# A gated long convolution and an MLP: the sequence in two halves, each transformed modulo x^1024 - i, with MLP pieces of the first half written between convolution pieces of the second

## The chip, the cores and the metric

The kernel runs on one core of a Trainium2 chip. The core has a matrix engine (TensorE, in the profile PE, with its weight loads as PEld), a vector engine (VectorE, DVE), a scalar engine (ScalarE, ACT), a general engine (GpSimd, POOL), an engine that mostly starts transfers (SyncE, SP), and 16 DMA engines. Each engine works through its own instruction list in order, and semaphores tie the lists together. Matrix products land in PSUM, eight banks of 128 x 512 fp32 values; everything else lives in SBUF, 128 partitions wide.

The metric is the device time of one launch in microseconds, as the median of several runs. The profile comes from one execution, of which it records the span from the first to the last instruction.

## The reference

The input sequence has S = 2048 positions of D = 512 channels. Two kinds of layer alternate, four layers in all, with a residual around each and a layer norm in front:

```
A(q, k, v): k_shift[s] = sum over t of k[s-t] * shift_k[:, 3-t..]   (4 taps per channel)
            kv = k_shift * v
            y  = causal convolution of kv with ssm_k (length 2048), by FFT of length 4096
            y  = y + kv * ssm_D
            return q * y
B(x):       h = gelu(layernorm(x) @ w1 + b1);  return h @ w2 + b2      (F = 1376)

x = A_q
x = x + A(layernorm(x), k, v);  x = x + B(layernorm(x))
x = x + A(layernorm(x), k, v);  x = x + B(layernorm(x))
```

k, v and the filters are the same in both A layers and do not depend on x, so y is computed once and used twice: an A layer is then only `x + layernorm(x) * y`. B normalises once more, so between two MLPs each row goes through two layer norms and one gating product.

## The kernel before

The convolution is written as a transform modulo x^2048 - i. A real sequence of 2048 values becomes 1024 complex ones of a twisted transform, which gives the causal (linear) convolution without padding. A transform of 2048 = 32 x 64 has two matrix stages: stage one multiplies by the table `Ft` (`first_stage`, L320, matmul L327), then 16 x 2 transposes per chunk of 128 channels turn the result (L344), and stage two multiplies by `Wt` (L381 for the filter, L448 for kv). The filter's spectrum lies in `ZK`, and a copy with real and imaginary halves swapped in `KSW`, made by eight SBUF-to-SBUF transfers of 512 KB (`sa..`, `sb..`). VectorE multiplies the spectra (pieces `T`, L459, two products at once in a 128 x 2048 instruction), TensorE goes back with the table `Mt` (pieces `V`, L471), transposes (pieces `TP`, L515) and `GPt` (pieces `Y`, L493) into `YA`. A sequence chunk cc is 128 of the 512 channels; filter pieces are named K, those of kv U, X, T, V, TP and Y.

In front of this k is transposed (pieces `kT`, L405), and the 4-tap shift is done as matmuls against diagonal matrices `DG` (pieces `kv`, L421, 32 matmuls for 8 rows x 4 taps; pieces `kvm` multiply by v, L427). The diagonals are made on GpSimd (pieces `dg0` to `dg3`, L398, 16 instructions in all) from the tap table `sF`, a cast of `sT`, which a small transfer on ScalarE's queue brings (L194). The filter is transposed into token order too (pieces `KT`, L367).

The MLP works on groups of 512 positions (GT = 4 rows of 128), four groups per layer. `mm1` (L609) does 11 x 4 matmuls of 512 columns into one PSUM bank after the other, each emptied by a gelu on ScalarE (L617) into `hT`; `mm2` (L619) does 4 x 11 matmuls, each result added to x by VectorE (L628); in the last layer each row tile is then stored. `prep` (L283) does the layer norm, gating and second layer norm of a later group on VectorE and GpSimd, writes the result to DRAM from the GpSimd queue (L293) and reads it back transposed on the SP queue (L294) into `lnT`.

The order of the convolution and of the layer norms of the first two groups is a list written out by hand, `ORDER`: each word is a piece, its engine (P TensorE, D VectorE, A ScalarE, G GpSimd, S the SP queue) and its buffer numbers. `_Plan.write` emits the pieces in that order; each engine runs its own pieces in the order of the list. `p0` to `p3` are four PSUM tiles of two banks. After the list comes the MLP in plain loops, over groups 0 to 7 in the order mm1 of group i, `prep` of group i + 2, mm2 of group i - 1:

```
for i, (l, g) in enumerate(seq):
    mm1(ns[i])
    if i < len(seq) - 2:
        ns[i + 2] = prep(seq[i + 2][1])
    ...
    if prev is not None:
        mm2(ns[prev], seq[prev][1], seq[prev][0] == 1)
    prev = i
```

A transfer from the SP or ScalarE queue counts on one of eight semaphores, in turn, so the ninth such transfer waits until the first has landed.

Of the kernel before, what the change touches and what calls it, by code (L numbers as in the profile page):

```python
# [17 lines left out]
KT2.P1 dt1.D K1S0.P20 KT2e.D KT3.P3 K1S0e.A dg2.G dt2.D K1S1.P0 KT3e.D K1S2.P1 K2S0.P21 K1S2e.A KT0.P3 K1S1e.D  # L20
K2S0e.A dt3.D K2S3.P1 KT0e.D K2S2.P0 K2S3e.A kT0.P2 dt0.D K2S2e.A K2S1.P3 kT0e.D kT3.P1 K2S1e.A K3S0.P02 kT3e.D
kT1.P2 K3S0e.A K3S1.P3 kT1e.D K3S2.P1 K3S1e.A K2T0.P0 K3S2e.A K1S3.P2 K2T0e.D K2T1.P3 K1S3e.A K3S3.P1 K2T1e.D
K0S0.P01 K3S3e.A K1T0.P2 K0S0e.D K0S1.P3 K0S3.P1 K0S1e.A K1T0e.D K1T1.P0 K0S3e.A K0S2.P3 K1T1e.D K3T0.P2 kT2.P1
K0S2e.D K3T1.P0 kT2e.A lM.S K3T0e.D K0T0.P3 K3T1e.D K210.P2 kv21.P1 K210e.A K0T0e.D K200.P0 kvm21.D K216.P2
K200e.A kv30.P3 K216e.A K217.P1 kvm30.D K213.P0 K217e.A kv20.P2 K213e.A K211.P3 kvm20.D K202.P1 kv00.P0 K202e.A
K211e.D K201.P2 kvm00.D kv01.P1 K201e.A U0S0.P30 kvm01.D K203.P0 U0S0e.A U0S1.P2 K0T1.P1 K203e.D U0S1e.A U0S3.P3
K0T1e.D sa00.S U0S2.P0 sb00.S U0S3e.A kv10.P2 U0S2e.D K212.P1 kvm10.D K204.P3 K212e.A U2S0.P02 K207.P2 U2S0e.D
K204e.A U0T0.P1 sb10.S sa10.S K207e.A K215.P3 U0T0e.D K214.P0 kv31.P2 K214e.A K215e.D K205.P1 sa11.S kvm31.D
sb11.S U2S1.P0 K205e.A U0T1.P3 U2S1e.A X00.P20 U0T1e.D K206.P1 X00e.A X01.P01 K206e.D U2S3.P3 kv11.P2 X01e.A
T00.D0 sa01.S U2S3e.A sb01.S U2S2.P1 T01.D1 V00.P01 U2S2e.A X02.P32 kvm11.D V00e.A V01.P1 X03.P20 X02e.A V01e.D  # L30
U2T0.P0 X03e.A U3S0.P30 U2T0e.D U2T1.P1 U3S0e.A U3S3.P2 U2T1e.D X20.P01 U3S3e.A U3S2.P3 U3S1.P1 X20e.D U3S2e.A
U1S0.P22 U1S0e.D U1S2.P0 U3S1e.A U1S3.P3 U1S1.P1 U1S2e.A T20.D2 U3T0.P2 U1S1e.A T03.D0 X22.P01 U1S3e.A U3T1.P1
U3T0e.D V20.P30 X22e.A U3T1e.D V03.P2 V20e.A X30.P00 T22.D1 V03e.A U1T0.P1 T02.D2 X30e.A X23.P31 U1T1.P2 X23e.A
U1T0e.D V02.P0 U1T1e.D X31.P32 V02e.A V22.P1 T30.D0 X31e.A lx.S TP00.P2 V22e.A T23.D2 X13.P00 V30.P32 X13e.A
T31.D1 X11.P11 V23.P0 V30e.A TP00e.D X11e.A X21.P32 T13.D0 V31.P2 X21e.A Y00.P1 T11.D2 V23e.A X33.P30 T21.D1
V31e.A X32.P01 TP08.P2 X32e.A s10.D Y00e.A X10.P02 X10e.A V21.P1 TP08e.A T10.D1 s11.G X12.P02 s00.D X33e.A
V10.P21 X12e.A Y08.P3 V10e.A V11.P0 Y08e.A V13.P2 T12.D1 s01.G V11e.A V21e.D V12.P3 V13e.A T32.D2 TP20.P0 V12e.A
T33.D0 V32.P1 TP10.P2 TP20e.D V32e.A w1.S w3.S w2.S w4.S V33.P3 TP10e.D Y20.P1 V33e.A s02.D Y10.P0 Y20e.A
TP30.P2 TP18.P3 Y10e.A TP30e.D TP28.P1 s12.A ga.D Y30.P2 TP34.P0 gs.D Y30e.A TP18e.A TP38.P2 gl0.D TP34e.A
Y18.P3 gl2.D TP38e.A gp00.G Y34.P0 Y34e.D gp02.G gb00.A h2.D Y38.P0 gb02.D Y18e.A LT00.P2 h0.D LT00e.A LT02.P3  # L40
LT02e.A hs2.D TP28e.A hs0.D gp12.G Y38e.A Y28.P2 gb12.A gp10.G Y28e.D gb10.A
"""
NA, NB = 32, 64
# [8 lines left out]
def _make_tables():  # L52
    a = np.arange(NA)
    k1 = np.arange(NA)
    psi = 2 * np.pi * np.outer(a, k1 + 0.25) / NA

    F = np.zeros((128, 2, 128))
    G = np.zeros((128, 2, 128))
    for x in range(2):
        for bh in range(2):  # L60
            rows = 4 * a + 2 * bh + x
            F[rows, x, bh * 64:bh * 64 + 32] = np.cos(psi)
            F[rows, x, bh * 64 + 32:bh * 64 + 64] = np.sin(psi)
            for i, p in enumerate(rows):
                G[bh * 64:bh * 64 + 32, x, p] = np.cos(psi[i]) / 64
                G[bh * 64 + 32:bh * 64 + 64, x, p] = np.sin(psi[i]) / 64
    b = np.arange(NB)
    k2 = np.arange(NB)
    W = np.zeros((128, NA, 128))
    M = np.zeros((128, NA, 2, 128))  # L70
    for k in range(NA):
        phi = 2 * np.pi * (((k + 0.25) * b / 2048)[:, None] + np.outer(b, k2) / NB)
        c, s = np.cos(phi), np.sin(phi)
        for bh in range(2):
            cb, sb = c[bh * 32:bh * 32 + 32], s[bh * 32:bh * 32 + 32]
# [12 lines left out]
    W = W[32 * (p % 4) + 16 * (p // 4 % 2) + p // 8]
    GP = G[32 * (p % 4) + p // 4]
    return tuple(_to_bf16_uint16(t) for t in (F, G, GP, W, M))  # L90


class _Plan:
# [3 lines left out]
    def __init__(self, rings):  # L97
        self.rings = rings
        self.items = []

    def add(self, name, cost, deps, fn, take=(), free=(), nbytes=0, last=0):
        it = dict(name=name, cost=cost, deps=[d for d in deps if d is not None], fn=fn, take=list(take), slot={},
                  free=list(free), nbytes=nbytes, last=last)
        self.items.append(it)
        return it

    def write(self, order):
        pieces = {it["name"]: it for it in self.items}
        assert len(pieces) == len(self.items)
        for word in order.split():  # L110
            name, how = word.split(".")
            it = pieces.pop(name)
            it["eng"] = how[0]
            it["slot"] = {ring: int(c) for ring, c in zip(it["take"], how[1:])}
            it["fn"](it)
        assert not pieces
# [3 lines left out]
def kernel(ctx: ExitStack, tc: tile.TileContext, A_q, A_k, A_v, A_shift_k, A_ssm_k, A_ssm_D,  # L120
                 B_x, B_w1, B_b1, B_w2, B_b2, out):
    nc = tc.nc
# [4 lines left out]
    NT = S // P  # L127
# [3 lines left out]
    TOK = "(p nt) d -> p nt d"  # L131
    q_d, k_d, v_d, out_d = (t.flatten_outer_dims() for t in (A_q, A_k, A_v, out))
    K = 1024
    NZT, NTB = 3, 3
# [5 lines left out]
    F_np, G_np, GP_np, W_np, M_np = _make_tables()  # L140
    F_h = nc.inline_tensor(F_np, name="tabF")
    G_h = nc.inline_tensor(G_np, name="tabG")
    GP_h = nc.inline_tensor(GP_np, name="tabGP")
    W_h = nc.inline_tensor(W_np, name="tabW")
    M_h = nc.inline_tensor(M_np, name="tabM")

# [4 lines left out]
    ROW = 149 * K // 2  # L151
# [3 lines left out]

        return apf(arena, p0 * ROW + off // 2, [[ROW, n]] + dims)

    def place(name, shape, off):
# [7 lines left out]
    ZK = place("ZK", [P, 2, NA, D // 2], 0)  # L166
    ZX = place("ZX", [P, 2, NA, D // 2], 32 * K)
# [37 lines left out]
    def chunk(t, c):  # L205

        return t[:, c // 2, :, c % 2 * CW:c % 2 * CW + CW]
# [469 lines left out]
```

## Time and profile before

| | |
|---|---|
| median of three runs | 278.88 us (278.71 to 278.91) |
| span of the profiled execution | 277.7 us |
| TensorE busy | 257.6 us, 93% of the span, 2208 matmuls |
| VectorE busy | 187.0 us, 67% |
| ScalarE busy | 153.8 us, 55% |
| GpSimd busy | 41.1 us, 15% |
| data moved by DMA | 27.48 MB |

The profiled execution lasted 277.7 us from its first to its last instruction, and the median of the runs is 1.2 us above that span. In the page's slices a digit is the busy share of a fortieth of the span (6.9 us) in tenths; PEclk is the granted clock of TensorE in tenths of full speed. A row of the chain of waits is start, duration and what ran; because the matmuls are pipelined, the durations in the chain are paces, while the mean of a single matmul in the groups is its latency. A row of the table of stages gives the stage, its length, the busy time of each engine with the number of instructions, the granted clock, the share of DMA time and the rate. A row of the timeline is start, duration, engine, line, operation, tiles and count, with the idle time before it in brackets.

### The profile page before, as it was taken

Reading aid. Unit: us, or ns where it says so; the run is one execution under the profiler, and the core shown is the slowest. Engines: PE = TensorE matmul, PEld = TensorE weight load, DVE = VectorE, ACT = ScalarE, POOL = GpSimd, SP = SyncE. Lnnn points to the kernel's source line nnn. Section 1 sums busy time; section 2 is a strip of 40 time slices with the busy share of each in tenths; the row PEclk is TensorE's granted clock in tenths of the full one; section 3 lists DMA queues with packets and bytes.
Section 4 is the critical chain, followed back from the end, with each engine's and each line's share of the span. In section 5 each row is a group of like instructions: output and inputs, shape, how many; then the busy total and the mean of one; then the engine's idle time right before and its main releaser. Section 6 shows DMA issues by size and latency. Waiting matters only on the chain.

```text
span 277.7 us, 5353 instructions
## 1 busy us (share of the span) xinstructions
PE 257.6 (93%) x2208; PEld 168.6 (61%) x2208; DVE 187.0 (67%) x346; ACT 153.8 (55%) x186; POOL 41.1 (15%) x73
## 2 busy tenths in 40 slices
PE   3979999999997994589999999999999999999994
PEld 3969999998997994535444444444444444444441
DVE  0959767799999999995857875886777720110221
ACT  1566655788899889798751713705507217036000
POOL 3490000000002402313020121111111200000000
PEclk9999999999999999779999999999999999999999
DMA  7993703994800083000523023023040070110111
GB/s 234 308 402 148 293 14 76 225 216 94 304 2 2 2 295 113 1 2 9 143 76 78 0 77 76 4 76 76 2 130 21 6 210 13 38 38 2 39 55 58
DMA packets 21164, 27.48 MB, mean 99 GB/s; under 512 B 13874, under 2 KB 17684, under 8 KB 19988
## 3 DMA queue, kind: packets, MB, share of 16 engines
q1 hardware_dynamic: 19522, 23.93, 29.2%
q0 software_dynamic: 944, 3.15, 3.5%
q8 instruction: 17, 0.28, 0.4%
q10 hardware_dynamic: 674, 0.07, 0.2%
q14 instruction: 7, 0.06, 0.1%
HBM read 14.56 MB, written 5.24 MB: 71 GB/s over the span
## 4 chain that ended last, share of the span: by engine, by line
PE 76%; DVE 13%; DMA 5%; ACT 2%; issue 2%; ACTq 0%; POOL 0%; DVEq 0%
PE po L625 27%; PE ph L615 26%; DMA sT<-in_A_shift_k_dram 3%; PE p_121 L421 3%; DMA arena<-in_A_k_dram 2%; PE p_120 L344 2%; DVE lst_105 L241 2%; DVE T_95 L459 2%; PE p_121 L344 1%; PE p_119 L344 1%; PE p_120 L421 1%; PE p_122 L327 1%; PE p_122 L344 1%; DVE arena L535 1%; DVE arena L427 1%
## 5 line engine op out<-in xcount | busy, mean ns | idle before, releaser
L617 ACT ACTIVATE arena<-ph,B_73 128x512 bf16<-128x512 f32 (+1 forms) x88 | 60.2, 687 | 71.0 <-PE ph L615 71.0
L615 PE MATMUL ph<-arena 128*128 128x512 bf16 (+1 forms) x352 | 79.1, 385 | 1.1 <-ACT arena L617 1.1
L625 PE MATMUL po<-arena 128*128 128x512 bf16 (+1 forms) x352 | 77.7, 379 | 0.0
L615 PEld LDWEIGHTS <-arena 128*128 128x128 bf16 (+1 forms) x352 | 35.6, 101 | 43.3 <-issue 3.6
L625 PEld LDWEIGHTS <-arena 128*128 128x128 bf16 (+1 forms) x352 | 34.3, 98 | 40.9
L628 DVE TENSOR_TENSOR arena<-po,arena 128x512 bf16<-128x512 f32 x32 | 22.0, 687 | 50.8 <-PE po L625 50.8
L421 PEld LDWEIGHTS <-arena 128*128 128x128 bf16 x256 | 15.0, 98 | 0.2
L223 ACT ACTIVATE arena<-p_120 128x1024 bf16<-128x1024 f32 (+1 forms) x8 | 10.0, 1248 | 6.5 <-PE p_120 L381 4.7
L327 PEld LDWEIGHTS <-arena 128*128 128x128 bf16 x128 | 11.9, 99 | 1.9 <-issue 0.4
L225 DVE COPY arena<-p_119 128x2048 bf16<-128x2048 bf16 x6 | 7.3, 1221 | 7.8 <-PE p_119 L367 6.7
L493 PEld LDWEIGHTS <-GPt 128*128 128x128 bf16 x128 | 8.0, 102 | 6.5 <-issue 3.8
L241 DVE BATCH_NORM_STATS2 lst_105<-arena 128x6 f32<-128x512 bf16 (+2 forms) x20 | 11.2, 579 | 0.3
L223 ACT ACTIVATE arena<-p_121 128x1024 bf16<-128x1024 f32 (+3 forms) x8 | 9.5, 1187 | 3.3 <-PE p_121 L381 1.7
L225 DVE COPY arena<-p_121 128x2048 bf16<-128x2048 bf16 (+1 forms) x9 | 10.4, 1160 | 1.0 <-PE p_121 L515 0.6
L241 DVE BATCH_NORM_STATS2 lst_109<-arena 128x6 f32<-128x512 bf16 x16 | 10.8, 685 | 0.3
L225 DVE COPY arena<-p_120 128x2048 bf16<-128x2048 bf16 x7 | 8.6, 1221 | 3.0 <-PE p_120 L405 2.0
L596 POOL MEMSET arena<- 1x512 bf16 x2 | 1.0, 519 | 61.5 <-PE p_122 L448 61.5
L241 DVE BATCH_NORM_STATS2 lst_101<-arena 128x6 f32<-128x512 bf16 x16 | 9.9, 679 | 0.1
L241 DVE BATCH_NORM_STATS2 lst_97<-arena 128x6 f32<-128x512 bf16 x16 | 9.9, 678 | 0.1
L250 POOL TENSOR_TENSOR lrs_107<-lrs_107,mhalf 128x4 f32<-128x4 f32 (+1 forms) x5 | 4.9, 975 | 33.5 <-DVE lnm_108 L247 33.5
L398 POOL TENSOR_SCALAR DG<-IDt,sF 128x128 bf16<-128x128 bf16 x16 | 9.3, 607 | 0.1
L250 POOL TENSOR_TENSOR lrs_103<-lrs_103,mhalf 128x4 f32<-128x4 f32 x4 | 5.0, 1246 | 26.8 <-DVE lnm_104 L247 26.8
(161 smaller groups left out, 400.5 us busy)
## 6 DMA issues: line engine op xcount, KB each, us to landing
arena<-arena SPq DMA_DIRECT2D x8, 512.0 KB, 8.3
arena<-in_A_ssm_k_dram SPq DMA_DIRECT2D x4, 512.0 KB, 5.0
arena<-in_A_k_dram SPq DMA_DIRECT2D x4, 512.0 KB, 7.1
arena<-in_A_v_dram SPq DMA_DIRECT2D x2, 1024.0 KB, 11.5
arena<-tabM SPq DMA_DIRECT2D x1, 2048.0 KB, 8.8
arena<-in_A_q_dram SPq DMA_DIRECT2D x1, 2048.0 KB, 8.1
out_dram<-arena SPq DMA_DIRECT2D x16, 128.0 KB, 1.7
arena<-in_B_w_dram SPq DMA_DIRECT2D x1, 1376.0 KB
```

What stands on the lines that cost most here:

```text
L223: nc.scalar.activation(dst, src, AF.Copy)
L225: nc.vector.tensor_copy(dst, src)
L241: nc.vector.bn_stats(self.st[:, i, h, :], x_t[:, GT * g + i, c0:c9])
L250: nc.gpsimd.tensor_tensor(self.rs[:, a:b], self.rs[:, a:b], mhalf[:, a:b], ALU.pow)
L327: nc.tensor.matmul(o[:, i, :], src[:, 4 * q + i, cs], Ft[:].rearrange("p x m -> p (x m)"), start=True, stop=True)
L344: nc.tensor.transpose(o[:, i, :], zk, IDt[:])
L398: nc.gpsimd.tensor_scalar(out=DG[:, ct, t, :], in0=IDt[:], scalar1=sF[:, ct, t:t + 1], scalar2=None, op0=ALU.mult)
L421: nc.tensor.matmul(o[:, i, :], w, DG[:, cc, t, :], start=t == 0, stop=t == KS - 1)
L615: nc.tensor.matmul(ph[0:m, :], W1t[:, ct, ft * P:ft * P + m], lt[:, ct, :], start=ct == 0, stop=ct == CT - 1)
L617: nc.scalar.activation(ht[0:m, ft, :], ph[0:m, :], AF.Gelu_apprx_tanh, bias=B1[0:m, ft:ft + 1])
L625: nc.tensor.matmul(po[:], ht[0:m, ft, i * P:(i + 1) * P], W2t[0:m, ft, :], start=ft == 0, stop=ft == FT - 1)
L628: nc.vector.tensor_tensor(xs, po[:], xs, ALU.add)
```

## The change

The sequence is cut into two halves of 1024 positions (h = 0, 1), and each half into rows `(p n)` with n = 8 for each of 128 partitions. All transforms are modulo x^1024 - i, of 1024 = 32 x 32. With halves K0, K1 of the filter and U0, U1 of kv, the first half of the output is the convolution of U0 with K0. The second half is U1 with K0 plus U0 with K1', where the transform of K1' takes in both K1 and K0 (a second table in `Ft` carries K0's part). So:

- stage one of the second filter half has two matmuls for each one of the first half (`terms`);
- for the first output half there is one product per piece (`T0..`), for the second two (`Ta1..` and `Tb1..`), and the way back (`V1..`) has 32 matmuls per piece instead of 16;
- the spectrum of U0 stays in SBUF (`X0`) for the second half;
- the transposes of the filter (`KT`), of k (`kT`), the shift (`kv`) and the rest keep their numbers, in other groupings; the order in which SP starts its loads is new, with half a tensor per load for k, v and the filter rows.

The whole kernel, the MLP included, is now in `ORDER`. An MLP group i has six pieces `m1i0` to `m1i5` (two blocks of 128 hidden channels with 8 matmuls of 512 columns into a PSUM tile of two banks; the sixth has one block), their gelus `gei0` to `gei5`, four pieces `m2i0` to `m2i3` (11 matmuls each) and their adds `rei0` to `rei3`. The groups run over 0, 1 of the first layer, 0, 1 of the second (these are the first half of the sequence), then 2, 3 of the first layer and 2, 3 of the second. Pieces of groups 0, 1 and 2 stand between the convolution pieces of the second half. The layer norms work on two row tiles at a time: `sa` (statistics, VectorE), `pa` (power, GpSimd), `aa` (apply, VectorE or ScalarE), `ga` (gating and add, VectorE), `sb`, `pb`, `ab` (the second norm). Group 0 is transposed on TensorE (`LT`); for the other seven the result goes out in two transfers `dw` and comes back transposed with `dr`, all three on the SP queue. `hT` has two places; groups 0, 1, 2, 3, 5 and 7 use one of them, 4 and 6 the other. In one of the statistics steps an algebraic form of the double norm is used (`twice`).

The instruction lists of the two kernels, on TensorE in matmuls by line (before to after): Ft stage one 128 (L327) to 160 (L342); its transposes 256 to 256; Wt 64 + 128 to 64 + 128; the way back 256 (L471) to 384 (L481); its transposes 128 to 128; Y 128 to 128; shift 256 to 256; filter transposes 64 to 64; k transposes 64 to 64; MLP 352 + 352 to 352 + 352; transposes of normalised rows 32 to 16. On VectorE the products with the filter go from 16 to 24.

The core of the diff:

```diff
 ORDER = """
-lK1.S dg3.G lK2.S lK3.S lG.S lH.S lK0.S lk1.S lk0.S lk3.S lv1.S lW.S lv0.S lk2.S dg0.G KT1.P0 KT1e.D dg1.G
...
+lk0.S lK01.S lK00.S lK03.S dg3.G lK02.S lv0.S lk1.S lG.S lK11.S lK10.S lW.S dg1.G lv1.S lM.S lK13.S lK12.S kT00.P0
+kT01.P1 dg2.G kT00e.A KT00.P2 kT01e.D KT01.P3 KT00e.A dg0.G kv03.P1 KT01e.D dt0.D dt1.D K01S0.P3 kvm03.D K03S0.P2
+K01S0e.A0 kv00.P0 K03S0e.D1 U03S0.P2 kvm00.D kT10.P3 U03S0e.A2 K01S1.P1 kT10e.D U03S1.P2 K01S1e.A KT10.P0 U03S1e.A
...
+X110.P1 U12Te.A2 X111.P3 Ta130.D1 m104.P2 X111e.D0 X110e.A1 m100.P0 aa10.D ge04.A Tb110.D2 X130.P2 ge00.A X131.P1
+ga10.D m103.P3 X131e.A1 sb10.D X130e.A2 m102.P1 ge03.A Tb130.D0 pb10.G m105.P2 ge02.A ab10.D V130.P3 sa12.D dw10.S
...
+m241.P2 re40.D pa62.G aa62.D ga62.D m154.P0 re41.D m151.P1 ge54.A sa60.D m152.P0 sb62.D ge51.A pa60.G aa60.A m153.P1
+pb62.G ge52.A ga60.D m150.P2 ge53.A sb60.D m155.P0 ge50.A ab62.D pb60.G ge55.A dw62.S m252.P0 ab60.A dw60.S m253.P2
+re52.D dr6.S m251.P0 re53.D sa72.D m250.P2 re51.D pa72.G aa72.A m161.P0 re50.D sa70.D m165.P2 ge61.A ga72.D m162.P1
+pa70.G ge65.A aa70.A sb72.D m163.P2 ge62.A ga70.D pb72.G m164.P0 ge63.A sb70.D ab72.A m160.P1 pb70.G ge64.A dw72.S
+ab70.D ge60.A dw70.S m263.P1 dr7.S m262.P0 re63.D st63.S m261.P1 re62.D st62.S m172.P0 re61.D st61.S m175.P1 ge72.A
...
-    TOK = "(p nt) d -> p nt d"
+    HALF = "(h p n) d -> h p n d"
...
+        def first_stage(name, terms, deps, dst, edeps=(), ring=None):
...
+                        for j, (src, cs, f) in enumerate(terms):
+                            nc.tensor.matmul(o[:, i, :], src[:, 4 * q + i, cs], Ft[:, f, :], start=j == 0, stop=j == len(terms) - 1)
...
+                terms = [(Ktok[h], cs, 0)] + ([(Ktok[0], cs, 1)] if h else [])
...
+                    prods = [("T", xe, 0)] if h == 0 else [("Ta", X0e[2 * cc + j], 1), ("Tb", xe, 0)]
...
+                        n = 2 * len(tms)
+                        for i in range(8):
+                            for s in range(n):
+                                nc.tensor.matmul(o[:, i, :], Tb[tms[s // 2]["slot"]["T"]][:, s % 2, i, :], Mt[:, k0 + i, 1 - s % 2, :],
+                                                 start=s == 0, stop=s == n - 1)
...
+        seq = [(0, 0), (0, 1), (1, 0), (1, 1), (0, 2), (0, 3), (1, 2), (1, 3)]
+        HB = [0, 0, 0, 0, 1, 0, 1, 0]
+        VIA = "PDDDDDDD"
...
+                    dws.append(add(f"dw{i}{a}", "S", [ab], lambda it, d=d, ln=ln, a=a, b=b: queue(it["eng"]).dma_start(
+                        d[a * P:b * P, :].rearrange("(i p) d -> p i d", p=P), ln[:, a:b, :]), nbytes=2 ** 18))
...
+                pe = add(f"m1{i}{j // 2}", "P", trs + [w1], mms, take=["ps"], after=hfree, units=16 * len(fts))
...
+                pe = add(f"m2{i}{t}", "P", ge + w2 + [ones[HB[i]]], mms, take=["ps"], units=44)
...
-        for i, (l, g) in enumerate(seq):
-            mm1(ns[i])
-            if i < len(seq) - 2:
-                ns[i + 2] = prep(seq[i + 2][1])
```

More of the change, by code (lines that the diff above doesn't have):

```diff
@@ L99, in __init__, with add @@
         self.items = []
[L101 to L103 removed]
+    def add(self, name, engines, deps, fn, take=(), free=(), after=(), **info):
+        it = dict(name=name, engines=engines, deps=[d for d in deps if d is not None], fn=fn, take=list(take),
+                  slot={}, free=list(free), after=list(after), info=info)
@@ L187 @@
     mhalf = const.tile([P, 4], F32, name="mhalf")
+    Dc = place([P, D], 150.5 * K)[0:1, :]
     nc.gpsimd.memset(IDt[:], 1.0)
```

788 lines of the change are left out of this document (369 added, 419 removed).

## The prediction

> **What bounds the kernel now.** I read the page's slices first, then a table of stages, then the chain of waits, and last the timeline at the start and where the convolution ends.
>
> ```profile
> span 277.7 us, 5353 instructions
> PE   3979999999997994589999999999999999999994
> DVE  0959767799999999995857875886777720110221
> PEclk9999999999999999779999999999999999999999
> ```
>
> TensorE is full from the third slice on, but for a hole around slices 14 to 18. Where VectorE shows a row of nines TensorE still runs.
>
> ```profile
> 6.90:16.30 9.40, 7.77 (x90) 6.87 (x88) 7.85 (x10) 5.82 (x6) 5.47 (x11) 1.00 0.98 324
> 16.30:67.00 50.70, 50.40 (x721) 48.07 (x722) 40.23 (x34) 34.08 (x35) 4.20 (x8) 1.00 0.64 183
> 67.00:95.00 28.00, 26.24 (x426) 25.43 (x426) 27.92 (x40) 26.70 (x29) 5.33 (x6) 1.00 0.21 77
> 85.00:123.30 38.30, 28.77 (x380) 24.74 (x380) 37.47 (x94) 34.45 (x38) 10.03 (x15) 0.91 0.23 75
> 123.30:274.10 150.80, 150.70 (x708) 69.18 (x707) 82.55 (x195) 61.51 (x91) 18.26 (x28) 1.00 0.20 56
> 274.10:277.70 3.60, 0.00 (x0) 0.00 (x0) 0.66 (x1) 0.00 (x0) 0.00 (x0) 1.00 0.11 36
> ```
>
> Each row gives PE, PEld, DVE, ACT and POOL busy. The MLP stage from 123.3 us has no hole: 150.70 of 150.80 us. The hole lies in 85 to 123.3 us, where VectorE (37.47 of 38.30) does the first layer norms and gating. So TensorE bounds the kernel, and two things can shorten it: less work on TensorE, or fewer holes.
>
> **TensorE's work, before and after.** Pieces pass at these paces in the chain:
>
> ```profile
> 17.42 0.44 PE p_119 L327 x4
> 17.86 0.89 PE p_121 L405 x16
> 22.91 1.01 PE p_121 L344 x16
> 30.57 1.79 PE p_120 L421 x32
> 70.98 0.89 PE p_122 L471 x16
> 150.45 9.50 PE ph L615 x44
> 159.95 9.51 PE po L625 x44
> ```
>
> That is 0.0558 us for a matmul of 128 columns (1.79 / 32), 0.063 for a transpose with strided weights (1.01 / 16), 0.11 for 256 columns, 19.01 for one MLP group. Before: 864 matmuls of 128 columns 48.2, 448 strided transposes 28.3, 192 of 256 columns 21.1, eight groups 152.1, together 249.7 us. After: 976 give 54.5, 448 give 28.3, 224 give 24.6, the MLP 152.1, together 259.5 us. The two additions are the 128 extra matmuls of the way back (7.1) and the 32 extra of stage one (3.5); 16 transposes fewer give 0.9 back. TensorE thus has 9.8 us more to do.
>
> Before, 277.7 - 249.7 leaves 28.0 us without work: 3.6 after the last matmul and 24.4 of holes and slow clock. The end is unchanged (last add, last store), 3.6 us. So the change wins only if its holes stay under 24.4 - 9.8 = 14.6 us, the wait for the first data included.
>
> **The start.** This is where I find the largest new hole.
>
> ```profile
> 4.71 1.93 PE L367 MATMUL p_119<-IDt,arena 128*128 128x128 bf16 x16 [4.71 <-DMA arena<-in_A_ssm_k_dram]
> 6.44 1.91 PE L367 MATMUL p_120<-IDt,arena 128*128 128x128 bf16 x16
> 8.84 1.16 PE L367 MATMUL p_122<-IDt,arena 128*128 128x128 bf16 x16
> 10.73 0.20 POOL L200 CAST sF<-sT 128x16 f32<-128x16 bf16 x1 [7.47 <-DMA sT<-in_A_shift_k_dram]
> 11.03 9.33 POOL L398 TENSOR_SCALAR DG<-IDt,sF 128x128 bf16<-128x128 bf16 x16
> 0.80 0.36 ACTq L192 DMA_DIRECT2D Ft<-tabF  x1
> Ft<-tabF ACTq DMA_DIRECT2D x1, 64.0 KB, 3.3
> 1.85 8.82 DMA sT<-in_A_shift_k_dram
> sT<-in_A_shift_k_dram ACTq DMA_DIRECT2D x1, 4.0 KB, 8.8
> q10 hardware_dynamic: 674, 0.07, 0.2%
> ```
>
> The tap table sT is 4 KB but lands only at 10.7 us (1.85 + 8.82), and GpSimd then needs 9.33 us for the four diagonals, to 20.4 us. Before, the first shift matmul stands at 30.57 us, so this costs nothing. In the new list kv03, which needs dg3 (made first), is TensorE's fifth piece, and kv00, which needs dg0 (made fourth and last), its eighth. TensorE cannot pass kv00, and everything stands behind it.
>
> When does sT land now? ScalarE's queue carried 674 packets, nearly all of Ft (128) and sT (512 runs of 8 bytes), so some 8 and 32 on each of 16 DMA engines. From Ft's landing at 4.1 us (0.80 + 3.3) to 10.7 are 6.6 us, 0.206 us a packet. At 324 GB/s an engine moves 20.2 KB per us, so 4 KB, one row of the filter loads then on the SP queue, takes 0.20 us. An sT packet thus seems to wait for one SP packet each time. (That is my reading of the numbers; no row shows the turns.) In the new list SP's packets are eight of 8 KB per engine (lk0, 0.40 us each) beside Ft, then 32 of 2 KB (the four filter loads, 0.10 us each) beside sT: 2.2 + 3.2 + 3.3 = 8.7 us. I take 8.8. The cast and its gap took 0.34 us (10.69 to 11.03); the diagonals are ready at 8.8 + 0.34 + 9.33 = 18.5 us. Bounds: 4.5 us if sT no longer waits for other packets (just behind Ft's 4.1), giving 14.2, and 10.7 as before, giving 20.4.
>
> TensorE meanwhile has kT00, kT01 (0.89 each), KT00, KT01 (1.05 each, with the slow first 32 partly hidden), kv03 (from 11.5, when dg3 is there; 1.79) and two stage-one pieces (0.44 each), 6.5 us in all, done at about 14.2. It stands still for 4.3 us, and from 18.5 us has 259.5 - 6.5 = 253.0 us to go.
>
> After a long pause the first matmuls are slow: the first 16 above took 6.44 - 4.71 = 1.73 us, later ones about 1.05. Kept up for 32 matmuls that is 1.4 us. I take 1.0, between 0 (before, TensorE was held up in 85 to 123 us with a mean clock still at 0.91) and 1.7. The Trainium skill, "TensorE: Matmul & The Clock Gate", Part 1, says that after one idle window of about 3.4 us the clock is halved until about 3.4 us of work have passed. By it the term would be an estimated 1.7 us in place of 1.0, and the sum 0.7 higher; the trace's 1.73 against 1.05 at the start agrees.
>
> The eight transfer semaphores make lK11 and all later loads wait for sT. By then 4 MB stand in the queue, over 12 us of work at 324 GB/s, so that costs nothing; without this cover it would cost the 2 us or so of a landing.
>
> **The mixed stage.** The hole of 85 to 123 us goes: VectorE's norms now run while TensorE does the second half's convolution and the first groups' MLP. What is late next is VectorE itself.
>
> ```profile
> 77.22 1.21 DVE L459 TENSOR_TENSOR T_94<-xb_91,arena 128x2048 bf16<-128x2048 bf16 x1
> 116.55 1.28 DVE L241 BATCH_NORM_STATS2 lst_109<-arena 128x6 f32<-128x512 bf16 x2
> 113.84 0.68 DVE L535 TENSOR_TENSOR arena<-arena 128x1024 bf16<-128x1024 bf16 x1
> 112.45 0.73 DVE L259 TENSOR_SCALAR arena<-arena,lrs_107,lnm_108 128x512 bf16<-128x512 bf16 x2
> 274.07 0.69 DVE arena L628
> ```
>
> From V031 to m132 the list gives TensorE 109.5 us. VectorE has 35 products and evacuations (1.21), 21 pairs of statistics (1.55 with their small steps), 11 gatings (1.25), 11 adds (0.69) and 12 applies (0.65): 104 us, 95%. The nearest rows are the stage 16.3 to 67 us, where TensorE lacks 0.30 of 50.7 us (0.6%), and 67 to 95 us with VectorE at 100%, where it lacks 1.76 of 28.0 (6.3%). On 109.5 us these are 0.7 and 6.9 us. I take 2.0, nearer the lower, since MLP pieces of 1.73 and 2.38 us lie between and need VectorE less. The eight swap transfers and the weights lie behind one another on SP, but each has ten to twenty us of other pieces ahead of its first use; I cost them at nothing and let them share the upper end.
>
> **The gelus at the end of mm1.**
>
> ```profile
> 122.59 2.49 ACT L617 ACTIVATE arena<-ph,B_73 128x512 bf16<-128x512 f32 x4
> 119.76 1.52 ACT L257 ACTIVATE arena<-arena,lnm_112,lrs_111 128x512 bf16<-128x512 bf16 x2 [0.58 <-POOL lnm_112 L251]
> 116.65 0.70 POOL L250 TENSOR_TENSOR lrs_111<-lrs_111,mhalf 128x2 f32<-128x2 f32 x1 [0.99 <-DVE lnm_112 L247]
> 201.75 0.80 POOL L293 DMA_DIRECT2D lnd_113<-arena  x1 [1.71 <-DVE arena L259]
> 205.20 1.56 SPq L294 DMA_TRANSPOSE arena<-lnd_113  x1
> arena<-lnd_113 SPq DMA_TRANSPOSE x2, 4.2
> ```
>
> Before, mm2 of the previous group stood between mm1 and mm2 of a group and hid the gelus. Now m252 stands right behind m15's last piece, and m263 right behind m16's. A pair of gelus takes 1.24 us (2.49 / 2), and between them ScalarE must apply norms of the next groups (1.52 a pair). For group 5, counting from m154's start: ge51 at 3.6, aa60 to 6.4, then ge52, ge53, ge50 and ge55 to 10.7, while TensorE is through at 9.5: 1.3 us. For group 6, from m161's start: ge61 and ge65 to 3.8, aa70 (waiting on GpSimd) to 5.2, ge62, ge63 to 7.7, ab72 to 9.1, ge64, ge60 to 11.7, while TensorE is through at 9.5: 2.3 us. Together 3.6; between 2.6 and 5.1 if ScalarE is 0.5 us earlier or 0.75 later each time.
>
> The way out and back through DRAM took 205.20 - 201.75 = 3.45 and then 4.2 us, 7.7 in all, and stands now seven times on SP. For group 7 from dw70 (some 19.9 us behind the last mm2 piece before it) that is 27.6, against 28.4 when m172 is due; other groups have 0.2 to 2 us to spare. I cost it at nothing; it shares the upper end of the mixed stage. Stores behind `dr` on SP wait with it, but only the last four end the kernel. GpSimd loses six transfer issues and gains smaller norm steps; it has room (41 us).
>
> **Sum.** 18.5 + 253.0 + 1.0 + 2.0 + 3.6 + 3.6 = 281.7 us of span. The median stood 1.2 above the span (278.88 - 277.7): 282.9 us, 1.4% slower.
>
> **Rivals.**
> - *The cover holds (faster).* Nothing waits behind kv00, clock and start as above. For it speaks 0.30 us lacking in 50.7; against it the count for ScalarE. 281.7 - 5.6 = 276.1, with 1.2: 277.3 us. It decides for "faster" once the waits behind kv00 sum to less than 0.9 us in place of 5.6.
> - *The mixed stage is bound by VectorE and by transfers (slower).* For it: 95% load in a fixed order, and spare times of a few tenths in the DRAM way. With 6.9 in place of 2.0 and 1 us lost on the DRAM way: 288.8 us.
> - *sT is early (no change).* At 4.5 us the diagonals are ready at 14.2, no pause, full clock: 282.9 - 4.3 - 1.0 = 277.6, or 278.7 where TensorE's first pieces, which need 1 MB of k first, are 1.1 late. Against it: the 8.8 us of the row.
>
> **How the numbers follow.** Forecast 0.53, around 282.9; cover holds 0.10; VectorE-bound 0.25; early sT 0.12. The range reaches to the cover at 277.3 below and a little over the VectorE-bound case above: 277.3 to 290. A measurement of this kernel can tell about 0.2% from no change, so 278.3 to 279.4 counts as the same. Faster is the cover and a third of early sT, 0.14; same 0.06; slower 0.80, whose own range is 280 to 290.
>
> **What would show it.** POOL's diagonals ending near 18.5 us and TensorE idle before kv00's 32 matmuls for about 4 us; 259.5 us of matmul paces; no hole near 100 us, VectorE at nine tenths through the middle; idle of 1 to 3 us twice in the last 90 us, released by ScalarE's gelus; an end of 3.6 us. The forecast is wrong if kv00 starts before 15 us, or if holes behind it sum to under 1 or over 12 us.

## The result, and the profile after

The changed kernel takes 289.8 us (median of four runs, 288.94 to 291.28) against 278.79 us: 1.0405 times the time before, with a 95% interval of 1.0381 to 1.043. It is slower by 4.0%, where 1.4% was forecast (282.9 us); the time lies at the upper edge of the range, 277.3 to 290. The profiled execution lasted 288.9 us from first to last instruction (290.62 us as a run), against 281.7 forecast, so 7.2 us of span are to be found. Some executions run in a slower state of the chip; here and below a ratio leaves them out, a median does not.

The page of the changed kernel, its span and slices (a slice is 7.2 us here):

```profile
span 288.9 us, 5680 instructions
PE   1668999999999989999999999999999989979994
DVE  0323778997999997999998898970115855931021
PEclk9977999999999999999999999999999999999999
```

The hole of slices 14 to 18 is gone, as forecast. In its place stand four poor slices at the start, with a slow clock in the third and fourth, and two dents near the end. The table of stages (PE, PEld, DVE, ACT and POOL busy, clock, DMA share, rate) says the same in microseconds:

```profile
0.00:18.50 18.50, 8.29 (x88) 7.81 (x89) 2.84 (x4) 5.04 (x3) 7.04 (x20) 0.96 0.87 291
18.50:60.00 41.50, 39.49 (x502) 37.12 (x501) 29.85 (x26) 27.49 (x27) 5.72 (x11) 0.94 0.29 92
80.00:100.00 20.00, 19.48 (x285) 18.24 (x284) 19.68 (x40) 16.81 (x17) 2.65 (x6) 1.00 0.43 120
100.00:130.00 30.00, 29.01 (x260) 18.33 (x259) 27.70 (x52) 20.40 (x25) 6.74 (x8) 1.00 0.43 118
235.00:285.30 50.30, 47.85 (x220) 21.56 (x219) 17.91 (x42) 19.45 (x31) 4.57 (x9) 1.00 0.22 61
285.30:288.90 3.60, 0.00 (x0) 0.00 (x0) 0.56 (x1) 0.00 (x0) 0.00 (x0) 1.00 0.11 36
```

VectorE works 19.68 of 20 us from 80 on, but TensorE has 19.48 there and 29.01 of the next 30: in the middle TensorE keeps nearly all its time. The start in the timeline:

```profile
1.85 0.40 ACTq L246 DMA_DIRECT2D sT<-in_A_shift_k_dram  x1
6.13 3.60 PE L414 MATMUL p<-IDt,arena 128*128 128x128 bf16 x32 [6.13 <-DMA arena<-in_A_k_dram]
13.96 0.20 POOL L252 CAST sF<-sT 128x16 f32<-128x16 bf16 x1 [10.68 <-DMA sT<-in_A_shift_k_dram]
14.26 9.30 POOL L406 TENSOR_SCALAR arena<-IDt,sF 128x128 bf16<-128x128 bf16 x16
14.92 0.22 PE L429 MATMUL p<-arena 128*128 128x128 bf16 x1 [2.99 <-POOL arena L406]
16.66 2.97 PE L429 MATMUL p<-arena 128*128 128x128 bf16 x29 [0.36 <-POOL arena L406]
21.87 0.22 PE L429 MATMUL p<-arena 128*128 128x128 bf16 x1 [0.92 <-POOL arena L406]
23.61 3.08 PE L429 MATMUL p<-arena 128*128 128x128 bf16 x29 [0.36 <-POOL arena L406]
26.48 0.97 PE L342 MATMUL p<-Ft,arena 128*128 128x256 bf16 x4
```

The tap table sT is there at 13.9 us, not at the forecast 8.8. The diagonals take 9.30 us as forecast and end at 23.56; kv03 waits for the first four of them, kv00 for the last four, one matmul per diagonal, and passes TensorE on to the next piece at 26.48 us. From their start to that point its last 29 matmuls take 2.87 us (26.48 - 23.61), where they take 1.62 at the pace of the forecast (29 x 0.0558): the clock is slow, 0.54 of full speed between 23.61 and 26.5 us. The transfers, with KB and median time from issue to landing:

```profile
arena<-lnd SPq DMA_TRANSPOSE x7, 4.4
Ft<-tabF ACTq DMA_DIRECT2D x1, 128.0 KB, 4.3
sT<-in_A_shift_k_dram ACTq DMA_DIRECT2D x1, 4.0 KB, 12.1
```

TensorE's largest waits by releaser (total, times, longest), and the two pieces in the timeline where the L591 waits stand:

```profile
PE p L414 <- DMA arena<-in_A_k_dram: 6.1, 1, 6.1
PE p L429 <- POOL arena L406: 6.1, 8, 3.0
PE p L591 <- ACT arena L581: 3.2, 2, 2.1
PE p L458 <- ACT arena L581: 1.0, 1, 1.0
PE p L481 <- DVE arena L472: 0.6, 1, 0.6
PE p L429 <- ACT arena L264: 0.3, 1, 0.3
PE p L490 <- DVE arena L595: 0.2, 1, 0.2
```

```profile
235.21 9.67 PE L591 MATMUL p<-arena 128*128 128x512 bf16 x44 [1.12 <-ACT arena L581]
256.45 7.29 PE L591 MATMUL p<-arena 128*128 128x512 bf16 x33 [2.07 <-ACT arena L581]
```

The span adds up against the forecast like this. Up to the end of kv00: 26.48 us, forecast 21.3 (18.5 + 1.79 + 1.0 for the slow clock), so 5.2 more. From there to the last matmul at 285.30: 258.8 us, of which 251.2 are the paces of the work left (253.0 - 1.79); that leaves 7.6 us of waits and slow clock, forecast 5.6, so 2.0 more. The end is 3.60 us, as forecast. 5.2 + 2.0 = 7.2.

### The profile page after: what moved, and what is told of

Read it like the earlier page. It is cut to its first block, busy times and chain, and to the rows that moved or that the text cites. A ratio compares the mean times of both kernels' runs of the same rounds, so it can differ in the third digit from the quotient of the medians.

```text
span 288.9 us, 5680 instructions
## 1 busy us (share of the span) xinstructions
PE 267.4 (93%) x2352; PEld 179.1 (62%) x2352; DVE 192.2 (67%) x363; ACT 169.4 (59%) x203; POOL 52.8 (18%) x95
## 3 DMA queue, kind: packets, MB, share of 16 engines
q1 hardware_dynamic: 25698, 26.48, 30.8%
## 4 chain that ended last, share of the span: by engine, by line
PE 73%; DVE 8%; ACT 5%; POOL 3%; DMA 2%; issue 2%; ACTq 0%
PE p L591 25%; PE p L574 19%; PE p L342 6%; PE p L481 5%; PE p L350 5%; PE p L429 4%; DVE lst L285 3%; ACT arena L581 2%; PE p L458 2%; PE p L497 2%; PE p L490 2%; DMA arena<-in_A_q_dram 2%; POOL arena L406 2%; PE p L394 2%; DVE arena L472 2%
## 5 line engine op out<-in xcount | busy, mean ns | idle before, releaser
L264 ACT ACTIVATE arena<-p 128x1024 bf16<-128x1024 f32 (+2 forms) x81 | 90.6, 1172 | 43.2 <-PE p L342 22.1
L591 PE MATMUL p<-arena 128*128 128x512 bf16 (+1 forms) x352 | 78.0, 379 | 3.2 <-ACT arena L581 3.2
L581 ACT ACTIVATE arena<-p,B 128x512 bf16<-128x512 f32 (+1 forms) x88 | 54.7, 685 | 43.4 <-PE p L574 43.4
L574 PE MATMUL p<-arena 128*128 128x512 bf16 (+1 forms) x352 | 78.5, 379 | 0.0
L298 POOL TENSOR_TENSOR lrs<-lrs,mhalf 128x2 f32<-128x2 f32 x32 | 30.1, 942 | 183.3 <-DVE lnm L295 183.3
L591 PEld LDWEIGHTS <-arena 128*128 128x128 bf16 (+1 forms) x352 | 34.1, 98 | 43.8 <-ACT arena L581 2.4
L285 DVE BATCH_NORM_STATS2 lst<-arena 128x6 f32<-128x512 bf16 x64 | 41.0, 683 | 1.1 <-DMA arena<-in_A_q_dram 0.6
L305 ACT ACTIVATE arena<-arena,lnm,lrs 128x512 bf16<-128x512 bf16 x32 | 23.9, 806 | 16.2 <-POOL lnm L299 16.2
L266 DVE COPY arena<-p 128x2048 bf16<-128x2048 bf16 (+1 forms) x19 | 22.6, 1194 | 15.5 <-PE p L414 10.7
L472 DVE TENSOR_TENSOR arena<-arena 128x2048 bf16<-128x2048 bf16 x24 | 28.7, 1220 | 2.5 <-ACT arena L264 1.1
L266 DVE CAST arena<-p 128x1024 bf16<-128x1024 f32 x22 | 26.5, 1219 | 1.1 <-PE p L481 0.7
L429 PE MATMUL p<-arena 128*128 128x128 bf16 x256 | 19.1, 237 | 6.4 <-POOL arena L406 6.1
L481 PE MATMUL p<-arena 128*128 128x128 bf16 x384 | 23.6, 219 | 0.6 <-DVE arena L472 0.6
L481 PEld LDWEIGHTS <-arena 128*128 128x128 bf16 x384 | 22.3, 98 | 2.1 <-DVE arena L472 0.8
L342 PE MATMUL p<-Ft,arena 128*128 128x256 bf16 x160 | 22.1, 280 | 0.2 <-ACT arena L264 0.2
L429 PEld LDWEIGHTS <-arena 128*128 128x128 bf16 x256 | 17.4, 107 | 7.6 <-issue 7.6
L350 PEld LDWEIGHTS <-arena 128*128 128x128 bf16 x256 | 17.8, 148 | 0.4 <-ACT arena L264 0.2
L342 PEld LDWEIGHTS <-arena 128*128 128x128 bf16 x160 | 15.5, 101 | 2.5 <-issue 0.3
```

The source lines that it names most:

```text
L264: nc.scalar.activation(dst, src, AF.Copy)
L266: nc.vector.tensor_copy(dst, src)
L285: nc.vector.bn_stats(self.st[:, i, :], xg[:, i, :])
L298: nc.gpsimd.tensor_tensor(self.rs[:, a:b], self.rs[:, a:b], mhalf[:, a:b], ALU.pow)
L342: nc.tensor.matmul(o[:, i, :], src[:, 4 * q + i, cs], Ft[:, f, :], start=j == 0, stop=j == len(terms) - 1)
L350: nc.tensor.transpose(o[:, i, :], apf(zt(evs[0]), zt(evs[0]).offset + i, [[ROW, P], [NK, P]]), IDt[:])
```

## The experiments

The theory at this point: the start costs what is missing, because sT lands late and the diagonals stand before TensorE. The rivals: the mixed stage is the loss, bound by VectorE, or simply the 9.8 us of added matmuls.

**The tap table first on SP.**

```diff
-    nc.scalar.dma_start(sT[:], A_shift_k.rearrange(...))
+    nc.sync.dma_start(sT[:], A_shift_k.rearrange(...))
```

> The changed kernel with one edit: the tap table sT is loaded as the first transfer of the SP queue, not as the third of ScalarE's. Theory (the late taps cost what TensorE stands still in front of kv00, and the sum's start term was 5.4 us short): sT lands near 4 us in place of 13.9, the diagonals are ready near 14 in place of 23.6, kv00 runs at full clock; the median falls by 9 to 11 us, from 289.8 to 279 to 281. Rival (the pause in front of kv00 only covers work that VectorE or later loads hold up anyway): the diagonals come early all the same, but TensorE stands still later, and the median falls by less than 4 us.

Measured: 282.37 us (282.14 to 283.06), ratio to before 1.0149 [1.0116, 1.0183], 7.4 us less than the changed kernel; span 280.6, 8.3 less. Its timeline:

```profile
3.28 0.21 POOL L252 CAST sF<-sT 128x16 f32<-128x16 bf16 x1
3.59 9.30 POOL L406 TENSOR_SCALAR arena<-IDt,sF 128x128 bf16<-128x128 bf16 x16
12.61 1.95 PE L429 MATMUL p<-arena 128*128 128x128 bf16 x32
15.27 1.95 PE L429 MATMUL p<-arena 128*128 128x128 bf16 x32
246.44 8.98 PE L591 MATMUL p<-arena 128*128 128x512 bf16 x33 [2.06 <-ACT arena L581]
```

sT lands before 3.3 us in place of 13.9, nothing waits for a diagonal, and the piece behind kv00 starts at 17.06 us, 9.4 us earlier. The piece m263 starts 10.0 us earlier (246.44 against 256.45), so the start is passed on whole. The median fell by less than the expected 9 to 11 us and by more than the rival's 4. In the profile, what is missing is in that last row: after a wait as long as in the changed kernel (2.06 and 2.07 us) the same 33 matmuls took 8.98 us in place of 7.29, at a granted clock of 0.57 in their first 4 us (1.00 in the changed kernel). The start is the larger part of the loss: shown. That the rest is the mixed stage is not yet excluded.

**The same edit in the kernel before.**

> The kernel before with the same edit on sT alone. Theory (there the shift matmuls come at 30 us and the diagonals are ready at 20): the diagonals come 6 us earlier and nobody waits for them; but the SP queue stood 5.0 us on sT's semaphore before the last loads of k and v, so TensorE's wait of 1.7 us on k near 16 us may go: 0 to 2 us faster, 277 to 278.8 us. Rival (sT holds the kernel before as well): over 3 us faster.

Measured: 278.53 us (278.11 to 280.57), ratio 1.0005 [0.9984, 1.0026]. In the old order the late table was hidden by other work; the change made it a cost.

**Why does sT land so late?** Two runs on one chip: the taps read as 128 runs of 32 bytes in place of 512 runs of 8, and the changed kernel once more.

```diff
-    nc.scalar.dma_start(sT[:], A_shift_k.rearrange("(ct p) k -> p ct k", p=P))
+    nc.scalar.dma_start(sT[:], A_shift_k.rearrange("(p ct) k -> p ct k", p=P))
```

> The kernel after, with one edit: the tap table sT is loaded as 128 runs of 32 bytes in place of 512 runs of 8 bytes, at its old place, third on ScalarE's queue. The taps then go to the wrong channels (the first part of the computation that this changes; the time is that of the same work). Theory of turns (each packet of sT waits for one packet of the SP queue): 8 packets on a DMA engine in place of 32, so sT lands within about 4.5 us of Ft's landing even behind packets of 8 KB, at 5 to 8.5 us, the diagonals are ready at 15 to 18 us in place of 23.6, and the span is 4 to 6 us shorter than the kernel after's. Theory that the transfer waits for the loads that SP had issued before it, whatever its size: it lands at 11 to 14 us as before the edit, and the span stays within 1.5 us.

> The kernel after, unchanged, beside the run with contiguous runs and on the same chip, for the place where sT lands: it was 13.96 us in the profile after and 11.05 us in the run with only mm2's order changed. Theory of turns with a fixed pairing: 13.5 to 14.2 us again. If the place hangs on how the queues happen to interleave: anything from 10 to 14.5 us, and the span follows it one for one (288.9 us at 13.96).

Measured: one run each, 289.04 and 291.43 us, spans 287.3 and 289.7. With contiguous runs, in the timeline:

```profile
9.70 0.20 POOL L252 CAST sF<-sT 128x16 f32<-128x16 bf16 x1 [6.43 <-DMA sT<-in_A_shift_k_dram]
253.21 8.97 PE L591 MATMUL p<-arena 128*128 128x512 bf16 x33 [2.29 <-ACT arena L581]
```

and the changed kernel again:

```profile
12.47 0.20 POOL L252 CAST sF<-sT 128x16 f32<-128x16 bf16 x1 [9.20 <-DMA sT<-in_A_shift_k_dram]
255.59 8.98 PE L591 MATMUL p<-arena 128*128 128x512 bf16 x33 [2.30 <-ACT arena L581]
```

The unchanged kernel's table landed 1.5 us earlier than in the first profile, so there is no fixed pairing of packets from which the landing could be computed. With a quarter of the runs it was 2.8 us earlier still (9.70 against 12.47), which is one run of each; the number of small runs seems to count. But the landing lies between what the two theories gave, 5 to 8.5 and 11 to 14 us. Neither holds as written, and what sets the landing stays open. Both spans are longer than the earlier landing would give: m263 starts 0.9 and 3.2 us earlier than in the first profile (255.59 and 253.21 against 256.45), and then its 33 matmuls lose 1.7 us to a slow clock that the first profile did not have there.

**The waits for the gelus.** mm2 takes its 11 products in the order in which its group's gelus come, so that the last gelu is needed last:

```diff
+            fto = [f for w in ORDER.split() if w.startswith(f"m1{i}") for f in (2 * int(w[3]), 2 * int(w[3]) + 1) if f < FT]
...
-                    for ft in range(FT):
+                    for ft in fto:
...
-                        nc.tensor.matmul(o, ht[0:m, ft, t * P:t * P + P], W2t[0:m, ft, :], start=ft == 0, stop=ft == FT - 1)
+                        nc.tensor.matmul(o, ht[0:m, ft, t * P:t * P + P], W2t[0:m, ft, :], start=ft == fto[0], stop=ft == fto[-1])
```

> The changed kernel with one edit: each mm2 row tile adds its eleven products in the order in which the gelus of that group come, so that its first matmuls don't need the last gelu. Theory (the two waits on ScalarE's gelus before m252 and m263, 1.1 and 2.1 us in the profile, lie on the path): both vanish, the median falls by 2.5 to 3.5 us. Rival (what is saved there is lost at the next group's way through DRAM, whose result is due just then): the gelu waits vanish, a wait on a transposing transfer appears, and the time falls by less than 1 us.

Measured: 288.45 us (287.62 to 289.44), ratio 1.0375 [1.0333, 1.0417]. The two waits stayed, 1.12 and 2.06 us. The 3.0 us by which this span is shorter (285.9) is the start again: sT was there at 11.05 us, 2.9 earlier. So the data was not what m252 and m263 waited for alone. The list shows another tie: m252 takes the PSUM tile P0, which m155 filled and the last gelu, ge55, empties; m263 takes P1 after m160 and ge60.

Both mends so far together, and the diagonals in the order 3, 0, 2, 1 (`dg0` and `dg1` change places):

> Both edits together, and the diagonals are made in the order 3, 0, 2, 1 in which TensorE asks for them, not 3, 1, 2, 0. Theory: kv00's diagonal is ready near 9 us, before TensorE gets there, so nothing is left of the pause: 12 to 14 us at the start and 3 at the gelus, 273 to 276 us, faster than the kernel before by 1 to 2%. Rival (loads or VectorE take over): not under 279 us.

Measured: 283.26 us (280.62 to 283.55), ratio 1.0156 [1.0101, 1.0211]: no better than the table alone. The gelu waits stood at 1.12 and 2.07, the order of the diagonals gained nothing, since they were not waited for any more, and the first half of k came at 7.55 us in place of 6.62. The expectation of 273 to 276 rested on the data theory, and on 12 to 14 us at the start where the table had given 7.4; it fell with both.

Then the tile itself, with the table first and mm2 in the order of the gelus:

```diff
-... dw62.S m252.P0 ab60.A ...
+... dw62.S m252.P3 ab60.A ...
-ab70.D ge60.A dw70.S m263.P1 ...
+ab70.D ge60.A dw70.S m263.P3 ...
```

> The taps first, mm2's products in the order of the gelus, and in addition m252 and m263 write to the PSUM tile that the last mm1 pieces did not use. In the run with the order alone both waits stayed at 1.12 and 2.06 us. Theory (they wait for the PSUM tile that the last gelu empties, besides its data): with both gone the two waits vanish and with them the slow clock behind the second, 3.2 + 1.7 us; 282.4 becomes 277 to 278. Rival (the way through DRAM is due just then and takes over): 280 to 282.

Measured: 278.81 us (277.5 to 279.88), ratio 1.0004 [0.9982, 1.0025]. Its timeline:

```profile
223.70 9.68 PE L592 MATMUL p<-arena 128*128 128x512 bf16 x44
242.71 7.39 PE L592 MATMUL p<-arena 128*128 128x512 bf16 x33
250.58 9.67 PE L574 MATMUL p<-arena 128*128 128x512 bf16 x44 [0.48 <-DMA arena<-lnd]
```

Both waits are gone, and with them the slow clock: 7.39 us for the 33 matmuls. Against the table alone that is 3.6 us in the median and 4.7 in the span: 3.2 from the waits, 1.6 from the clock and 0.4 from further up, less the wait that comes next, 0.48 us for a transposed group from DRAM. The median lies 0.8 us above the expected 277 to 278; the profiled execution, at 277.64 us, lies inside. Whether the new tiles alone would do without the new order was not tried. For m263 the list speaks against it: in the old order its first product needs ge60, the last gelu piece of the group. ScalarE's last four gelus end there at 244.89 us in this trace, so the first of ge60's two is over at some 244.3 (an estimate), 1.6 us behind the 242.71 at which m263 starts. The kernel is now as fast as before, with all the added matmuls in it.

**Does TensorE's added work or VectorE's bind the middle?** From the kernel with the table first, one run leaves out the matmuls of one of the two products in the second half's way back (128 matmuls, 7.1 us), the other the gating multiplication of the layer norms (L542; VectorE's busy time goes from 192.1 to 181.5 us):

```diff
-                        n = 2 * len(tms)
+                        n = 2
+                        t9 = tms[-1]
...
-                                nc.tensor.matmul(o[:, i, :], Tb[tms[s // 2]["slot"]["T"]][:, s % 2, i, :], Mt[:, k0 + i, 1 - s % 2, :],
+                                nc.tensor.matmul(o[:, i, :], Tb[t9["slot"]["T"]][:, s % 2, i, :], Mt[:, k0 + i, 1 - s % 2, :],
```

```diff
-                    nc.vector.tensor_tensor(v, v, ya_all(h, n0 + a, n0 + b), ALU.mult)
```

> The kernel with the taps first on the SP queue (282.4 us), less the 128 matmuls that the way back of the second half has more than before: the products of the first half with the second half of the filter are still made on VectorE, but not added, so the second half of the output lacks them. Theory (TensorE's added work lies wholly on the path, 0.0558 us each): 7.1 us less, 275 to 276. Rival (in the mixed stage VectorE at 95% sets the pace, and TensorE's added matmuls fill its pauses): under 3 us less.

> The kernel with the taps first, less the 16 gating products of VectorE (the multiplication of the normalised rows by the convolution's output is left out, 0.6 to 0.69 us each, 11 of them in the mixed stage): VectorE has 7 us less to do there. Theory (TensorE bounds that stage): 0 to 1 us less than 282.4. Rival (VectorE bounds it): 4 to 7 us less.

Measured, without the matmuls: 282.07 us (280.13 to 284.89), ratio 1.0105 [1.0074, 1.0135], span 278.4; without the gating: 282.86 us (282.52 to 283.19), ratio 1.0146 [1.0129, 1.0163], span 281.5. The base has 282.37 and 280.6. Stages of the base, then without the matmuls, then without the gating:

```profile
100.00:130.00 30.00, 30.00 (x301) 20.66 (x300) 28.45 (x61) 18.52 (x24) 8.84 (x11) 1.00 0.26 73
130.00:160.00 30.00, 29.94 (x274) 19.48 (x273) 27.36 (x60) 21.45 (x28) 10.19 (x15) 1.00 0.14 36
```

```profile
100.00:130.00 30.00, 27.64 (x227) 17.03 (x226) 28.99 (x62) 19.32 (x24) 9.75 (x11) 1.00 0.26 71
130.00:160.00 30.00, 27.45 (x224) 16.54 (x222) 27.55 (x64) 20.75 (x28) 10.16 (x15) 1.00 0.14 36
```

```profile
100.00:130.00 30.00, 30.00 (x298) 20.37 (x296) 26.27 (x58) 18.65 (x24) 7.62 (x10) 1.00 0.25 73
```

In the base TensorE is full, 59.94 of 60 us, and VectorE's relief of 10.6 us gains nothing. Without the 7.1 us of matmuls TensorE has holes, 4.9 us in those 60, 3.4 of them behind VectorE and 0.7 behind a transposed group from DRAM; the longest in the timeline:

```profile
145.63 1.16 PE L491 MATMUL p<-IDt,arena 128*128 128x128 bf16 x16 [1.78 <-DVE arena L596]
```

VectorE is at 28.99 of 30. The timelines at m263 tell what is left of the 7.1 us, without the matmuls and, below it, without the gating:

```profile
246.00 7.29 PE L592 MATMUL p<-arena 128*128 128x512 bf16 x33 [2.07 <-ACT arena L582]
```

```profile
247.34 8.98 PE L590 MATMUL p<-arena 128*128 128x512 bf16 x33 [2.07 <-ACT arena L580]
```

Without the matmuls the piece starts 0.4 us earlier than in the base (246.44); the other 1.7 of the 2.2 us between the spans is the slow clock behind the wait, which this execution did not have. Without the gating it starts 0.9 us later, after a wait of 1.37 us for w1 near 93 us that the base did not have. By the ratios (1.0149, 1.0105 and 1.0146) leaving out the matmuls gains 0.4%, some 1.2 us, with intervals that overlap, and leaving out the gating nothing. So TensorE and VectorE share the bound of the middle: either alone can be relieved by 7 to 11 us with about 1 us or nothing gained. What relieving both would give was not tried, and of the 7.1 us some 1.7 that the holes do not account for were not taken apart. The rival that the added matmuls of the way back are the loss is refuted, since leaving them out brings back 0.4 us in the trace and some 1.2 by the ratios; so is the rival that VectorE's load alone is.

**The load of the gelu table.** In the changed kernel TensorE's wait of 0.96 us at 106.35 stood behind a table load of 1.28 us on ScalarE, in front of the first gelu:

```profile
103.74 1.28 ACT L581 ACT_TABLE_LOAD   x1
106.35 1.05 PE L458 MATMUL p<-arena,Wt 128*128 128x128 bf16 x16 [0.96 <-ACT arena L581]
```

A gelu of 128 x 4 values at the start puts the one load there:

```diff
+    warm = const.tile([P, 4], F32, name="warm")
+    nc.scalar.activation(warm[:], mhalf[:], AF.Gelu_apprx_tanh)
```

> As the run before, and ScalarE's table for gelu is loaded at the start by one small gelu on 128 x 4 values, not at the first gelu of the MLP (1.28 us on ScalarE, and a wait of 0.95 us on TensorE behind it). Theory: 0.9 to 1.5 us less than the run before, 276 to 277, faster than the kernel before. Rival (the wait is for the gelus themselves): no change.

> The kernel before, with the tap table first on SP and a gelu of 128 x 4 values at the start, so that the one table load of ScalarE lies there and not at 121.29 us, where TensorE waited 1.07 us at 123.33. If the gain of the last version of the new kernel (0.4% faster than before) comes from the change: this stays at the time before, 278.5 to 279. If it comes from the early table, which the old order can have too: 277.3 to 278.0, and the two orders are equal within 0.2%.

Measured: the new order with all mends 277.56 us (277.27 to 277.83), ratio 0.9956 [0.9941, 0.9971]; the old order with the table of taps first and the early gelu 277.83 us (276.95 to 278.16), ratio 0.9957 [0.9942, 0.9971]. Both gain 0.4% on the kernel before, and they cannot be told apart. In the new order TensorE's wait for ScalarE near 100 us is gone, and the median is 1.25 us below the run before; the two profiled spans are alike (276.1 and 275.9 us), with k 0.85 us later here (7.34 against 6.49). TensorE's slices of the new order, and of the old, on their pages:

```profile
PE   0999999999999999999999999999999999999994
```

```profile
PE   2999999999997994599999999999999999999994
```

The new order has one hole, the wait for k at the start (7.3 us); the old starts at 5.4 us and has its hole in slices 14 to 18. One pays 9.8 us of work for the hole, and the spans are 276.1 and 276.4 us.

**An earlier start.** Two filter loads ahead of k's on SP, and the first filter transposes ahead of k's:

```diff
-lk0.S lK01.S lK00.S lK03.S ...  kT00.P0 kT01.P1 dg2.G kT00e.A KT00.P2 kT01e.D KT01.P3 KT00e.A dg0.G kv03.P1 KT01e.D
+lK01.S lK00.S lk0.S lK03.S ...  KT00.P0 kT00.P1 dg2.G KT00e.A kT01.P2 kT00e.A KT01.P3 kT01e.D dg0.G kv03.P1 KT01e.D
```

> The mended version of the new kernel (tap table first, mm2 in the order of the gelus, two free PSUM tiles, early gelu table; 277.56 us) with two of the four filter loads ahead of the first half of k on SP, and the first piece of filter transposes ahead of the two pieces of k's. TensorE then starts when 0.5 MB has come in place of 1 MB: at about 4.8 us in place of 7.3. If the start binds: 1.5 to 2.5 us less, 275 to 276.2 us. If the later pieces of the first 20 us wait for the data or for VectorE instead: within 0.5 us of 277.6.

Measured: 280.1 us (279.23 to 280.78), ratio 1.0048 [1.0033, 1.0063]: slower by 2.5 us than without it, the opposite of what either theory gave. In the timeline, kv03 without the edit and, below it, the start with it:

```profile
13.74 1.95 PE L431 MATMUL p<-arena 128*128 128x128 bf16 x32
```

```profile
5.74 1.93 PE L371 MATMUL p<-IDt,arena 128*128 128x128 bf16 x16 [5.74 <-DMA arena<-in_A_ssm_k_dram]
11.03 3.59 PE L416 MATMUL p<-IDt,arena 128*128 128x128 bf16 x32 [3.36 <-DMA arena<-in_A_k_dram]
15.64 2.21 PE L431 MATMUL p<-arena 128*128 128x128 bf16 x32
```

TensorE starts 1.6 us earlier, but k, needed by the next two pieces and by kv03, is there at 11.03 in place of 7.34, and kv03 starts at 15.64 in place of 13.74. With the half megabyte put ahead of it, k comes 3.7 us later. That fits a start that is bound by when k lands.

## Why the prediction was wrong in size

By its own steps:

- *When sT lands: wrong, the step that failed.* Of the sum 2.2 + 3.2 + 3.3 the first two terms, up to Ft's landing at 5.4 us, were close (5.1, from 0.80 + 4.3). The term that was mis-sized is the 3.3 us for sT's 32 packets an engine behind the four filter loads, 0.10 us each: sT landed 8.8 us behind Ft, 13.95 against 5.1. The forecast had read the old trace's 0.206 us a packet as one SP packet per sT packet and then halved it for smaller SP packets. It was marked as a reading that no row showed, and its rows fit other readings as well: the old 0.206 taken over unchanged gives 5.4 + 6.6 = 12.0 us. Three profiles of the same place have 13.96, 12.47 and 11.05 us. The bound of 10.7 us "as before" was below all three: beside another list of loads the table can land later than before, and the range did not allow for that. This cost 5.1 of the 7.2 us. What sets the landing stays open.
- *Diagonals, and that TensorE cannot pass kv00: right.* 9.30 us, ending 23.56, and TensorE waiting for them eight times, 6.1 us in all. With the table early the wait and 9.4 us of the start are gone.
- *The slow clock after a pause: close at the start, missing later.* 1.0 us was taken; from start to start the 29 matmuls of kv00 lost 1.25 us (2.87 against 1.62) and those of kv03 1.15, which stood under the wait for kv00's diagonals. Late in the kernel a like loss, 1.7 us, came after waits of 2.06 to 2.30 us in some executions and not in others. The forecast had no term for it there.
- *TensorE's work, 259.5 us: close.* Behind kv00 the waits in the timeline are 5.5 of the 7.6 us. Some 0.4 of the rest is the slow clock from 26.5 to 30 us (0.89 on average there); the other 1.7, under 1% of 251.2, was not taken apart.
- *The mixed stage, 2.0 us: right in size, in part by luck.* Its waits are 0.55, 0.30, 0.23, 0.96 and 0.24, together 2.3 us, though the largest stood behind the load of the gelu table, which the old kernel has too (at 121.29 us) and which the forecast did not move with the gelus; without it they are 1.3. VectorE at nine tenths, no hole near 100 us: as written. The rival that this stage costs 6.9 us gave 288.8 us, next to the measured time, and is refuted: a right total from a wrong place.
- *The gelus, 1.3 + 2.3: 1.12 + 2.07.* The size was right. The reason was only half right: the product's data was named, but the waits stayed when the data was needed last, and went when the PSUM tile was changed too.
- *The DRAM way, the swap transfers and the loads that wait for sT at nothing, the end at 3.6: right.* TensorE never waited for the seven transposing reads (4.4 us each); SP stood 6.9 us on sT's semaphore, and TensorE waited for none of the loads behind it; 3.60 us at the end.
- *The signs of being wrong: none appeared.* kv00 started at 21.87 us, not before 15, and the holes behind it sum to 5.5 us, between 1 and 12. No sign stood for a table later than forecast, which is what happened.

The direction was right, for the reason given: a start that the old order hid. The trade that the forecast weighed, 9.8 us of work against the hole near 100 us, comes out even when both orders are mended (277.56 and 277.83 us). The 4%, 11.0 us, is not the price of the split but of where two things stand: in medians 7.4 us came back with the tap table and 3.6 with mm2's order and two PSUM tiles. The gelu table, 1 us, the old order pays as well.

## What to carry to other kernels

A tiny transfer issued beside megabytes of loads is not early because it is tiny: where a whole stage hangs on it, put it first on the queue, and cost it by a range that reaches above what the old trace shows. When an engine is seen waiting for a releaser, ask whether it waits for that engine's data or for the buffer that it empties; needing the data later does not move the second wait. Two engines that are both nearly full hide each other's savings: here taking work from either one alone gained about 1 us or nothing.

## What was not expected of the hardware

- The 4 KB transfer of the taps took 12.1 us from issue to landing third on ScalarE's queue, beside the loads on SP, 10.6 us in a second profile of the same kernel, 9.1 us in the run with mm2 in the gelus' order, 7.8 us with a quarter of the runs, and 2.4 us as the first on SP. No run shows why.
- The wait before m263 was 2.06 to 2.30 us in eight profiles. In five of them the 33 matmuls behind it took 8.97 or 8.98 us, in three 7.29, and waits of 2.06 and 2.07 us are in both sets. The Trainium skill, "TensorE: Matmul & The Clock Gate", Part 1, has the clock halved after about one idle window of 3.4 us, with windows that run on their own; these waits are shorter than that window. That the same wait does and does not bring the loss agrees with windows that are not tied to the kernel; that it comes after 2.1 us at all does not agree with a window that has to be idle whole.
